# Zero rows of the second MoE stored during the first, another place for the partial block of two-block lists, and a tile moved 2 KB up

## The chip, the cores and the metric

The kernel runs on one core of a Trainium2 chip. The metric is the time of one execution in microseconds on the device. Lower is better. The core has a matrix engine (TensorE, PE in the profile), a vector engine (VectorE, DVE), a scalar engine (ScalarE, ACT), a general engine (GpSimd, POOL) and a queue engine that issues most transfers (SyncE, SP). The engines run side by side, each in the order of its own instructions, and wait for each other and for transfers through semaphores.

## The reference

Three stages, each on the output of the one before, all in fp32:

```python
# attention: q, k, v are [8 batches, 8 heads, 576, 64]
k_p, v_p = means of k and v over groups of 8 positions      # 72 of each
out = softmax(q @ k_p.T / 8) @ v_p
x = out as [4608 rows, 512]
# first MoE, then second MoE: 8 experts, w1 [8, 512, 1024], w2 [8, 1024, 512]
logits = x @ w_gate            # the second MoE adds modality_bias[modality_id]
e = argmax(logits); gate = softmax(logits)[e]
y = gate * (relu(x @ w1[e]) @ w2[e])
```

Each row is computed by one expert, the one that its logits pick. With the inputs given, experts 0 to 7 of the first MoE get 1018, 55, 333, 239, 827, 724, 24 and 1388 rows. In the second MoE experts 4 and 5 get 2286 and 2322 rows, the others none.

## The kernel before, in words

**Attention** runs over 40 steps (8 batches of 4 tiles of 128 rows and one of 64). Each finished tile is scattered by GpSimd, a row at a time, into a DRAM array `XS[0]`: eight areas of `CAP` = 4864 rows, one for each expert. An expert's list starts 256 rows into its area, and the 256 rows in front are zero. SP issues the loads of q, k and v ahead of the steps, and between them, by `zero_front` (line 92), the stores of those zero rows: one store of 256 rows (516 KB) for each expert and each MoE, at every second step from step 8 on, the first eight for `XS[0]`, the next eight for `XS[1]` (lines 674 and 675). The framework orders accesses to one DRAM array: a scatter to `XS[0]` waits for zero stores to `XS[0]` that were issued before it, and a zero store waits for scatters before it. Scatters among themselves are declared independent (line 172).

**An MoE** works through blocks of 256 rows (`moe_body`, line 904). A block reads its rows from `XS`, transposes them on VectorE (`xpose`), and splits them into a high and a low part (`split_x`, ScalarE and GpSimd) in the tile `xT`, or `xF` for the first block of each MoE. The weights of an expert are split in the same way: w1 into `w1h` (ScalarE) and `w1l` (VectorE for pieces 0 and 1, GpSimd for 2 and 3), w2 into `w2h` and `w2l`. GEMM 1 (line 284) makes eight pieces of 128 columns of h, each from 12 matmuls (high by high, high by low, low by high), into three PSUM buffers of two pieces; ScalarE writes the high part `hh` of two pieces, VectorE the low part `hl` (line 288). GEMM 2 (line 1075) makes the output in two halves of 128 rows with 24 matmuls each. In the first MoE the output of a block is at once multiplied with the second gate's weights: one product on VectorE for each half and expert (line 1157), part of it in the next block; then GpSimd scatters the rows into `XS[1]`. Hence `XS[1]` is filled during the first MoE, from its second block on.

Blocks are numbered from 0 here. **The partial block** of a list is the last one by position, with `count mod 256` rows; the rest of its 256 rows are other rows of the area, masked. If it has 128 rows or fewer, it is a **half block**: only one half is computed, with other code (`gemm1_half`, line 253: 48 matmuls, eight transposes, four `hl` pieces at line 273, and then 24 matmuls).

**The order of blocks** comes from a table that VectorE makes at run time (`table`, line 779) from the counts. The list that was longest after five batches goes first (expert 0); its first block is block 0. The others follow by number. `off` (line 843) is the position within a list at which its partial block stands, 0 or 1: 1 for the first list and for each list of more than one block. The code of a block is the same for every place; branches on bits of the table choose the half or full code and the splits of new weights. So the instructions in the program don't show the order, the table does. For the first MoE:

| block | 0 | 1 | 2 | 3 | 4 | 5 | 6 | 7 | 8 | 9 | 10 to 11 | 12 to 14 | 15 | 16 | 17 | 18 to 21 |
|---|---|---|---|---|---|---|---|---|---|---|---|---|---|---|---|---|
| expert | 0 | 0 | 0 | 0 | 1 | 2 | 2 | 3 | 4 | 4 | 4 | 5 | 6 | 7 | 7 | 7 |
| rows | 256 | 256 | 250 | 256 | 55 | 256 | 77 | 239 | 256 | 59 | 256 | 256, 212, 256 | 24 | 256 | 108 | 256 |
| code | full | full | full | full | half | full | half | full | full | half | full | full | half | full | half | full |

**Weights** of the next list are loaded into one staging tile (`stage`, w1 in one part, w2 in the other) as soon as the splits of the present list have freed it: w1 by four transfers of 512 KB at the end of the block before a list's first (`wload(0, nxt)`), w2 by one of 2 MB in the list's first block (`wload(1, i)`). All of them, the row loads (`ahead`, for the block after the next) and the zero stores stand in one queue, SP's. Where the block before a change of weights is full, its own code splits the next w1 and w2 between its matmuls (`next_w1`, `next_w2`). Where it is a half block, the splits come behind its GEMM 1 and at the start of the next block: pieces 0 and 1 of w1, then 2 and 3, `w2h`, and `w2l` in the next block's code, ahead of its `xpose` (lines 1004 to 1007 and 1033).

**Tiles in SBUF** stand one after the other in each partition, in the order in which the code asks for them; tiles named `edge` are gaps. By that layout `xT` begins at byte 172,032 of a partition, `xF` at 129,024.

Of the kernel before, what the change touches and what calls it, by code (L numbers as in the profile page):

```python
# [7 lines left out]
F32 = mybir.dt.float32  # L8
F32R = mybir.dt.float32r
# [3 lines left out]
ALU = mybir.AluOpType  # L13
# [7 lines left out]
def attn_moe_moe(ctx: ExitStack, tc: tile.TileContext, q, k, v, wg1, w1a, w2a, ids, wg2, bias2, w1b, w2b, out):  # L21
    nc = tc.nc
    ctx.enter_context(tc.manual_schedule())
    P = 128
# [5 lines left out]
    E = wg1.shape[1]  # L30
    FF = w1a.shape[2]
    NC1 = DM // P
    NC2 = FF // P
    BK = 256
# [17 lines left out]
    ZF = 8  # L52
# [37 lines left out]
    WT = dp.tile([E, DM], F32, name="WT")  # L90

    def zero_front(m, e):
        nc.sync.dma_start(
            out=XS[m][e * CAP : e * CAP + BK].rearrange("(p s) w -> p (s w)", p=P).rearrange("p (a w) -> p a w", a=4),
            in_=zero[:].unsqueeze(1).broadcast_to([P, 4, BK * XW // P // 4]))


    run = [ct([P, E], F32, f"run{m}") for m in range(2)]
# [56 lines left out]
    def gate_b2(oh, rk, ns, m, ib, rows, go=now, sc=None):  # L155
        pa = gtile(sc, 16, ns, E, "pa")
        go(lambda: nc.vector.tensor_tensor(out=pa, in0=rk[:, 0:ns, :], in1=run[m][:].unsqueeze(1).broadcast_to([P, ns, E]), op=ALU.add))
        go(lambda: nc.vector.tensor_tensor(out=run[m], in0=run[m], in1=rk[:, ns, :], op=ALU.add))
        go(lambda: nc.vector.tensor_tensor(out=pa, in0=pa, in1=oh[:, 0:ns, :], op=ALU.mult))
        pf = gtile(sc, 3, ns, 0, "pf")  # L160
        go(lambda: nc.vector.tensor_reduce(out=pf, in_=pa, op=ALU.add, axis=AX.X))
        pos = sp.tile([P, ns], I32, name=f"pos{ns}", tag=f"pos{ns}")
        go(lambda: nc.vector.tensor_tensor(out=pos, in0=pf, in1=ib, op=ALU.add))  # L163

        def scatter():
            def put(src, s):
                i = nc.gpsimd.indirect_dma_start(  # L167
                    out=XS[m][:], out_offset=bass.IndirectOffsetOnAxis(ap=pos[0 : src.shape[0], s : s + 1], axis=0),
                    in_=src, in_offset=None, bounds_check=E * CAP - 1, oob_is_err=False,
                )  # L170
                for o in scat[m]:
                    tc.declare_no_dep(i.ins, o.ins, reason="every row is written once")
                scat[m].append(i)

            rows(put)

        go(scatter)

    scat = [[], []]

    def pick_first(m):
        cnt = sp.tile([P, E], F32, name="pfc", tag="pfc")
# [401 lines left out]
    for i in range(len(T) + 2):  # L584
# [29 lines left out]
        if live:  # L614
# [48 lines left out]
            if i == 6:  # L663
# [7 lines left out]
                nc.vector.tensor_scalar(out=aux[:, :, :, 2:3], in0=aux[:, :, :, 1:2], scalar1=-1.0, scalar2=1.0, op0=ALU.mult, op1=ALU.add)  # L671
                for m in range(2):
                    nc.vector.tensor_copy(out=run[m], in_=ebase)
            if i >= ZF and (i - ZF) % 2 == 0 and (i - ZF) // 2 < 2 * E:
                zero_front((i - ZF) // 2 // E, (i - ZF) // 2 % E)
            if s == 1 and b >= 1:
                nc.gpsimd.tensor_copy(out=xr[(b - 1) % 2][:, :, DM + 1 : DM + 4], in_=aux[:, b - 1])
            if s == 0 and more:
# [74 lines left out]
    mp = ctx.enter_context(tc.tile_pool(name="moe", bufs=1, reuse_waits="tile"))  # L753
    mq = ctx.enter_context(tc.tile_pool(name="moep", bufs=1, space=PSUM, reuse_waits="tile"))
    my = ctx.enter_context(tc.tile_pool(name="moey", bufs=1, space=PSUM, reuse_waits="tile"))
    mp.tile([P, 176], F32, name="edge2")
    xT = mp.tile([P, 2, NC1, BK], F32R, name="xT")
    ring = [xr[0][:, 2:4], xr[1][:, 0:2], xr[1][:, 2:4]]
    tail = [xr[0][:, 0:2], ring[1]]

# [12 lines left out]
    invt = [mp.tile([P, NB, 2], F32, name=f"invt{m}") for m in range(2)]  # L773
    tab = [mp.tile([P, 4, NB], I32, name=f"tab{m}") for m in range(2)]
    nbt = [mp.tile([P, 5], I32, name=f"nbt{m}") for m in range(2)]
    hrow = mp.tile([P, 2, 2, BK], F32, name="hrow")
    yo = mp.tile([P, 2, DM], F32, name="yo")

    def table(m):
# [15 lines left out]
        V = nc.vector  # L795
# [4 lines left out]
        nb_ = t8("t_nb")  # L800
# [39 lines left out]

        off = t8("t_of")
        pp = t8("t_pp")
        V.scalar_tensor_tensor(out=off, in0=nb_, scalar=1.0, in1=is0[m], op0=ALU.is_gt, op1=ALU.max)
        V.tensor_tensor(out=pp, in0=start, in1=off, op=ALU.add)
        pd = t8("t_pd")
        V.scalar_tensor_tensor(out=pd, in0=nb_, scalar=-1.0, in1=off, op0=ALU.add, op1=ALU.subtract)
# [57 lines left out]
    def moe_body(m, i, full, chgn, hchg, phchg, slots, gate_prev, g1=None):  # L904
# [201 lines left out]
            next_w2(2, 3)  # L1106

        gemm2(1)
        if i == 1:
            regs[m] = load_regs(m)  # L1110
        if m == 0 and i > 0:
# [35 lines left out]
    revp = plx[:, 6 * E : 7 * E]  # L1147
    gsp = plx[:, 8 * E : 512]
    xq2 = mp.tile([P, BK // QP, P], F32, name="xq2")
    mt2 = mp.tile([P, 2, 4], F32, name="mt2")  # L1150
    V = nc.vector
    V.tensor_copy(out=revp, in_=rev)
    V.tensor_copy(out=biasp, in_=bias_t)
# [174 lines left out]
```

## Time and profile before

| | us |
|---|---|
| runs | 1168.77, 1168.18, 1159.60 |
| median | 1168.18 |
| profiled execution | 1167.45 |
| its span | 1165.6 |
| TensorE busy | 1080.1 (93%) |
| VectorE busy | 689.7 (59%) |
| GpSimd busy | 465.6 (40%) |
| ScalarE busy | 375.5 (32%) |

The span is the time from the first to the last instruction of the profiled execution; a little lies outside it. Busy times are of one engine, and the engines overlap. Line numbers (L284) are those of the kernel before. "A <- B" in a wait says that A's instruction began when B's had ended. A granted clock (PEclk) of 1.00 is 2.4 GHz, one of 0.50 is 1.2 GHz. In the names of the waits an engine's name with a q is its sequencer, which runs branches. The first MoE's blocks 3 to 10 lie between 297.18 and 477.93 us, and its 22 blocks end at 736.2 us.

### The profile page before, as it was taken

How to read it: one execution, taken by the hardware profiler on the slowest of the kernel's cores; microseconds unless marked ns; L12 is line 12 of the kernel's file. 1: busy time of each engine (PE TensorE's matmuls, PEld its weight loads, DVE VectorE, ACT ScalarE, POOL GpSimd, SP SyncE). 2: the span in 40 equal slices, each digit the busy share in tenths (PEclk: the TensorE clock that was granted, in tenths of full speed). 3: DMA queues.
4: the chain of work that ended last, by engine and by line, in shares of the span. 5: the costliest groups of instructions: out<-in, count | busy, mean ns of one | idle time of the engine just before them, and what ended most of it. 6: DMA issues, size and time to landing. Idle time of an engine off the chain costs nothing. (4 is left out here: it accounts for less than half of the span.)

```text
span 1165.6 us, 24589 instructions
## 1 busy us (share of the span) xinstructions
PE 1080.1 (93%) x6997; PEld 962.1 (83%) x6997; DVE 689.7 (59%) x1888; ACT 375.5 (32%) x717; POOL 465.6 (40%) x497
## 2 busy tenths in 40 slices
PE   7999989889988789999979998899999999999997
PEld 5888878778877678889768887888899899899996
DVE  4766676797897997898887777562212232212211
ACT  2454346332452432332622223222122242212221
POOL 6766887752372552351642234111211242221211
PEclk9999999989989899999989999999999999999999
DMA  8879999426285662171513621154111121121120
GB/s 214 216 194 227 252 288 272 171 57 164 57 227 156 167 183 62 38 205 39 155 63 74 167 65 39 41 139 137 54 58 38 40 63 48 37 65 47 38 66 32
DMA packets 148617, 135.61 MB, mean 116 GB/s; under 512 B 62502, under 2 KB 116774, under 8 KB 148272
## 3 DMA queue, kind: packets, MB, share of 16 engines
q1 hardware_dynamic: 138448, 104.68, 36.0%
q0 software_dynamic: 9424, 28.47, 6.8%
q8 instruction: 80, 1.31, 0.5%
q14 instruction: 137, 1.12, 0.3%
q10 hardware_dynamic: 528, 0.02, 0.0%
HBM read 249.30 MB, written 39.31 MB: 248 GB/s over the span
## 5 line engine op out<-in xcount | busy, mean ns | idle before, releaser
L284 PE MATMUL ph<-xT,w1h 128*128 128x256 f32 x2112 | 389.9, 288 | 25.0 <-DVE hl L288 14.7
L284 PEld LDWEIGHTS ph<-xT,w1h 128*128 128x128 f32 x2112 | 338.9, 197 | 31.6 <-DVE hl L288 15.7
L284 PE MATMUL ph<-xT,w1l 128*128 128x256 f32 x1056 | 303.8, 288 | 12.9 <-DVE w1l L228 11.2
L288 DVE SCALAR_TENSOR_TENSOR hl<-ph,hh 128x512 fp32r<-128x512 f32 x140 | 95.1, 685 | 266.0 <-ACT hh L287 230.2
L1075 PE MATMUL py<-w2h,hl 128*128 128x512 f32 x608 | 239.0, 393 | 8.5 <-DVEq L933 3.6
L1075 PE MATMUL py<-w2h,hh 128*128 128x512 f32 x608 | 240.0, 395 | 2.3 <-DVEq L933 1.2
L1075 PE MATMUL py<-w2l,hh 128*128 128x512 f32 x608 | 238.0, 391 | 0.6 <-POOL w2l L251 0.6
L241 POOL TENSOR_TENSOR xT<-xt,xT 128x512 fp32r<-128x512 f32 x78 | 101.6, 1321 | 335.8 <-ACT xT L240 335.4
L284 PEld LDWEIGHTS ph<-xT,w1l 128*128 128x128 f32 x1056 | 206.1, 195 | 14.0 <-DVE w1l L228 11.8
L1157 DVE SCALAR_TENSOR_TENSOR xr<-py,mt,wgt 128x512 f32<-128x512 f32 x284 | 195.4, 746 | 7.1 <-DVEq L933 6.6
L287 ACT ACTIVATE hh<-ph 128x512 fp32r<-128x512 f32 x140 | 83.6, 598 | 296.3 <-PE ph L284 262.4
L1075 PEld LDWEIGHTS py<-w2h,hl 128*128 128x128 f32 x608 | 114.6, 188 | 38.9 <-DVEq L933 5.3
L167 POOL DMA_INDIRECT XS<-xr,pos x84 | 83.4, 993 | 152.1 <-DVE pos L163 71.9
L1075 PEld LDWEIGHTS py<-w2h,hh 128*128 128x128 f32 x608 | 114.7, 189 | 24.7 <-DVEq L933 1.6
L1075 PEld LDWEIGHTS py<-w2l,hh 128*128 128x128 f32 x608 | 114.8, 189 | 22.9 <-POOL w2l L251 1.1
L1093 POOL DMA_INDIRECT out_dram<-yo,oi x37 | 37.2, 1005 | 132.2 <-POOLq L933 65.8
L335 POOL TENSOR_TENSOR stage<-stage 128x512 f32<-128x512 f32 (+4 forms) x60 | 70.3, 1182 | 15.2 <-DMA stage<-in_v_dram 8.0
L237 DVE STREAM_TRANSPOSE xt<-xq 128x1024 f32<-128x1024 f32 x42 | 52.2, 1244 | 38.1 <-POOL xT L241 19.8
L1091 ACT ACTIVATE yo<-py,mt 128x512 f32<-128x512 f32 x37 | 25.5, 690 | 146.5 <-PE py L1075 141.1
L1091 ACT ACTIVATE xr<-py,mt 128x512 f32<-128x512 f32 x39 | 26.8, 688 | 128.7 <-PE py L1075 121.9
L444 PE MATMUL psc<-kblk,qT 128*128 128x144 f32 (+1 forms) x320 | 52.8, 311 | 10.2 <-DVE asd L450 5.0
L228 POOL TENSOR_TENSOR w1l<-stage,w1h 128x1024 fp32r<-128x1024 f32 x22 | 53.9, 2470 | 6.9 <-ACT w1h L227 6.9
(291 smaller groups left out, 1352.2 us busy)
## 6 DMA issues: line engine op xcount, KB each, us to landing
stage<-in_moe_w_dram SPq DMA_DIRECT2D x196, 512.0 KB
stage<-in_moe_w_dram SPq DMA_DIRECT2D x44, 2048.0 KB
xq<-XS SPq DMA_DIRECT2D x180, 128.0 KB
XS<-zero SPq DMA_DIRECT2D x16, 516.0 KB
qp<-in_q_dram SPq DMA_DIRECT2D x32, 256.0 KB
stage<-in_k_dram SPq DMA_DIRECT2D x7, 1024.0 KB
stage<-in_v_dram SPq DMA_DIRECT2D x7, 1024.0 KB
wgt<-WT SPq DMA_DIRECT2D x1, 2048.0 KB
```

What stands on the lines that cost most here:

```text
L167: i = nc.gpsimd.indirect_dma_start(out=XS[m][:], out_offset=bass.IndirectOffsetOnAxis(ap=pos[0 : src.shape[0], s : s + 1], axis=0), in_=sr ...
L228: (eng or nc.vector).tensor_tensor(out=w1l[:, j], in0=wst1[:, :, f], in1=w1h[:, j].bitcast(F32), op=ALU.subtract)
L237: nc.vector.transpose(out=dst[:].rearrange("p c (g i) -> p g c i", i=QP), in_=src[:].rearrange("p g (c j) -> p g c j", c=NC1))
L241: (eng or nc.gpsimd).tensor_tensor(out=dst[:, 1, cs], in0=src[:, cs], in1=dst[:, 0, cs].bitcast(F32), op=ALU.subtract)
L284: nc.tensor.matmul(ph[:, fc % 2, :], lhsT=lw[:, fc // 2, c, fs], rhs=rx, start=n == 0, stop=n == len(mms) - 1)
L287: nc.scalar.activation(out=hh[f2], in_=ph, func=AF.Relu)
L288: nc.vector.scalar_tensor_tensor(out=hl[f2], in0=ph, scalar=0.0, in1=hh[f2][:].bitcast(F32), op0=ALU.max, op1=ALU.subtract)
L335: (eng or nc.gpsimd).tensor_tensor(out=r[0:pp, sl, 0:w], in0=r[0:pp, sl, 0:w], in1=r[0:pp, sl, w : 2 * w], op=ALU.add)
L444: nc.tensor.matmul(ps[0:tk, hp // 2, (hp % 2) * 2 * KP : (hp % 2 + 1) * 2 * KP], lhsT=qT[:, hp, 0:tk], rhs=kb[:, hp, :], start=True, stop= ...
L1075: nc.tensor.matmul(py, lhsT=lw[fc // 2][:, fc % 2, s * P : (s + 1) * P], rhs=rw[fc // 2][:, fc % 2, :], start=n == 0, stop=n == 3 * NC2 - 1)
L1091: nc.scalar.activation(out=x2[:, s, 0:DM], in_=py, func=AF.Copy, scale=t_[:, s, 0:1])
L1157: V.scalar_tensor_tensor(out=junk[e % 2], in0=py, scalar=sc, in1=wgt[:, e, :], op0=ALU.mult, op1=ALU.mult, accum_out=lgz[:, s, e : e + 1])
```

## The change

Three things. The zero stores for `XS[1]` leave attention: blocks 2 to 9 of the first MoE issue one each, behind the first half of GEMM 2 in the code. Those for `XS[0]` are issued at every third step from step 8 on. Zero stores and scatters are declared independent of each other, since no row is written by both. In the table `off` is 1 only for the first list and for lists of more than two blocks (the first list's own first block is not counted). And the small tile `mt2` is asked for earlier, the gap `edge2` shrinks from 176 to 160 elements and stands behind the small tiles, and `xT` behind it, so that `xT` begins at byte 174,080; the tiles behind it move by 32 bytes.

```diff
     def zero_front(m, e):
-        nc.sync.dma_start(
+        i = nc.sync.dma_start(
             out=XS[m][e * CAP : e * CAP + BK].rearrange("(p s) w -> p (s w)", p=P).rearrange("p (a w) -> p a w", a=4),
             in_=zero[:].unsqueeze(1).broadcast_to([P, 4, BK * XW // P // 4]))
+        for o in scat[m]:
+            tc.declare_no_dep(i.ins, o.ins, reason="no row is put in front of an expert's list")
+        zer[m].append(i)
+
+    scat = [[], []]
+    zer = [[], []]
...
-                for o in scat[m]:
+                for o in scat[m] + zer[m]:
                     tc.declare_no_dep(i.ins, o.ins, reason="every row is written once")
...
-    scat = [[], []]
...
-            if i >= ZF and (i - ZF) % 2 == 0 and (i - ZF) // 2 < 2 * E:
-                zero_front((i - ZF) // 2 // E, (i - ZF) // 2 % E)
+            if i >= ZF and (i - ZF) % 3 == 0 and (i - ZF) // 3 < E:
+                zero_front(0, (i - ZF) // 3)
...
-    mp.tile([P, 176], F32, name="edge2")
-    xT = mp.tile([P, 2, NC1, BK], F32R, name="xT")
...
+    mt2 = mp.tile([P, 2, 4], F32, name="mt2")
+    mp.tile([P, 160], F32, name="edge2")
+    xT = mp.tile([P, 2, NC1, BK], F32R, name="xT")
...
-        V.scalar_tensor_tensor(out=off, in0=nb_, scalar=1.0, in1=is0[m], op0=ALU.is_gt, op1=ALU.max)
+        V.scalar_tensor_tensor(out=off, in0=nb_, scalar=2.0, in1=is0[m], op0=ALU.is_gt, op1=ALU.max)
...
         gemm2(1)
+        if m == 0 and 2 <= i < 2 + E:
+            zero_front(1, i - 2)
...
-    mt2 = mp.tile([P, 2, 4], F32, name="mt2")
```

With the counts above the new table of the first MoE differs from the old one in blocks 5 and 6 alone: block 5 is expert 2's half block of 77 rows, block 6 its full block. The table of the second MoE is the same. The code of the blocks stands in the same order as before but for the zero stores.

SP's queue in attention, around the second zero store. `XS_86` is `XS[0]`, `zero` the tile of zeros, `qp` a q tile; a semaphore `DMASW` is that of a scatter, `DMAHW` that of an earlier transfer of SP's own. Before:

```order
L93 DMA XS_86<-zero 512x1x258 [waits DMAHW6_49]
L416 DMA qp<-in_q_dram 64x8x64 [waits DMAHW7_49,PE_49]
L416 DMA qp<-in_q_dram 128x8x64 [waits DMAHW0_49,PE_49]
L324 DMA stage<-in_v_dram 128x4x512 [waits DMAHW1_49,Pool_49]
L325 DMA stage<-in_v_dram 64x1x512 [waits DMAHW2_49,Pool_49]
L93 DMA XS_86<-zero 512x1x258 [waits DMAHW3_49,DMASW4_49]
```

With the change:

```order
L93 DMA XS_86<-zero 512x1x258 [waits DMAHW6_49]
L420 DMA qp<-in_q_dram 64x8x64 [waits DMAHW7_49,PE_49]
L420 DMA qp<-in_q_dram 128x8x64 [waits DMAHW0_49,PE_49]
L328 DMA stage<-in_v_dram 128x4x512 [waits DMAHW1_49,Pool_49]
L329 DMA stage<-in_v_dram 64x1x512 [waits DMAHW2_49,Pool_49]
L420 DMA qp<-in_q_dram 128x8x64 [waits DMAHW3_49,PE_49]
L93 DMA XS_86<-zero 512x1x258 [waits DMAHW4_49]
```

The second zero store comes one q tile later, and its wait for a scatter is gone.

SP's queue at the end of block 3 of the first MoE: the last of the four transfers of w1, and the row loads (`xq`) of block 4's code. `XS_87` is `XS[1]`. Before:

```order
L210 DMA stage<-in_moe_w_dram 32x4x1024
L1116 REGISTER_ALU
L1116 COMPARE_AND_BRANCH
L933 UNCONDITIONAL_BRANCH x4
L202 TENSOR_LOAD tab_2936
L202 ISA x2
L233 ISA
L233 DMA xq_79<-XS_86 32x8x128
```

With the change:

```order
L214 DMA stage<-in_moe_w_dram 32x4x1024
L93 DMA XS_87<-zero 512x1x258
L1123 REGISTER_ALU
L1123 COMPARE_AND_BRANCH
L938 UNCONDITIONAL_BRANCH x4
L206 TENSOR_LOAD tab_2926
L206 ISA x2
L237 ISA
L237 DMA xq_79<-XS_86 32x8x128
```

A zero store stands between the load of w1 and the row loads; the codes of blocks 2 to 9 each got one at this place.

## Rows read from the trace of the kernel before

**Rows 1.** Busy times of attention's stretch: from:to, length, engines (instructions), PEclk, DMA share, GB/s.

```profile
0.00:210.90 210.90, 190.45 (x1351) 163.26 (x1351) 137.12 (x441) 96.23 (x253) 153.96 (x233) 0.99 0.92 236
```

**Rows 2.** Waits of TensorE and SP from 0 to 211 us: in total, times, longest.

```profile
PE psc L444 <- DVE asd L450: 5.0, 3, 1.7
...
PE pq L429 <- DMA qp<-in_q_dram: 0.8, 1, 0.8
...
SPq L93 <- DMA XS<-xr,pos: 36.6, 3, 15.6
```

**Rows 3.** Busy times (PE, PEld, DVE, ACT, POOL) of blocks 3 to 8, 10 and 16.

```profile
297.18:319.59 22.41, 22.41 (x148) 20.32 (x147) 19.26 (x58) 10.91 (x15) 9.19 (x7) 1.00 0.12 27
319.59:333.21 13.62, 12.78 (x84) 10.78 (x83) 13.18 (x32) 8.62 (x15) 8.50 (x6) 1.00 1.06 277
333.21:368.20 34.99, 27.33 (x148) 24.80 (x148) 30.47 (x70) 10.08 (x15) 17.09 (x11) 0.85 0.72 204
368.20:381.82 13.62, 12.78 (x84) 10.79 (x83) 10.72 (x30) 8.50 (x15) 4.29 (x4) 1.00 0.16 38
381.82:415.94 34.12, 26.23 (x147) 22.59 (x148) 30.75 (x70) 14.18 (x19) 20.50 (x13) 0.90 0.66 160
415.94:441.17 25.23, 22.91 (x148) 20.21 (x147) 23.29 (x62) 6.80 (x11) 10.66 (x7) 1.00 0.76 209
455.02:477.93 22.91, 22.35 (x148) 20.05 (x148) 17.63 (x66) 4.42 (x9) 6.65 (x7) 1.00 0.27 78
581.15:617.37 36.22, 26.77 (x147) 24.24 (x148) 30.18 (x71) 10.67 (x16) 17.07 (x11) 0.86 0.26 84
```

**Rows 4.** TensorE's timeline in blocks 5 and 7: start, length, instruction, [idle <- releaser].

```profile
337.21 0.58 PE L284 MATMUL ph<-xT,w1l 128*128 128x256 f32 x1 [3.52 <-DVE w1l L228]
...
352.63 0.50 PE L284 MATMUL ph<-xT,w1h 128*128 128x256 f32 x2 [4.13 <-DVE hl L288]
...
386.07 0.58 PE L284 MATMUL ph<-xT,w1l 128*128 128x256 f32 x1 [3.78 <-DVE w1l L228]
...
399.31 0.52 PE L284 MATMUL ph<-xT,w1h 128*128 128x256 f32 x2 [2.42 <-DVE hl L288]
```

**Rows 5.** VectorE's timeline in blocks 3 to 5, and its products from the page.

```profile
307.48 2.36 DVE L228 TENSOR_TENSOR w1l<-stage,w1h 128x1024 fp32r<-128x1024 f32 x2 [0.24 <-ACT w1h L227]
...
326.73 1.60 DVE L273 TENSOR_TENSOR hl<-pt,hh 128x256 fp32r<-128x256 f32 x4
...
334.42 6.06 DVE L228 TENSOR_TENSOR w1l<-stage,w1h 128x1024 fp32r<-128x1024 f32 x2 [0.22 <-issue]
...
343.94 6.90 DVE L251 TENSOR_TENSOR w2l<-stage,w2h 128x1024 fp32r<-128x1024 f32 x2 [0.90 <-DVEq L1116]
350.77 1.23 DVE L237 STREAM_TRANSPOSE xt<-xq 128x1024 f32<-128x1024 f32 x1
...
L1157 DVE SCALAR_TENSOR_TENSOR xr<-py,mt,wgt 128x512 f32<-128x512 f32 x284 | 195.4, 746 | 7.1 <-DVEq L933 6.6
```

**Rows 6.** Timelines of SP at the end of block 3 and of ScalarE around 333.

```profile
317.37 2.87 SPq L210 DMA_DIRECT2D stage<-in_moe_w_dram  x4
...
330.70 3.89 ACT L227 CAST w1h<-stage 128x1024 fp32r<-128x1024 f32 x4 [2.00 <-DMA stage<-in_moe_w_dram]
...
337.87 3.89 ACT L244 CAST w2h<-stage 128x1024 fp32r<-128x1024 f32 x4 [2.70 <-DMA stage<-in_moe_w_dram]
```

**Rows 7.** Busy times behind the two stops in block 5.

```profile
337.20:343.30 6.10, 6.09 (x28) 6.09 (x29) 5.54 (x16) 4.49 (x5) 3.64 (x3) 0.50 0.25 49
353.70:357.00 3.30, 3.30 (x18) 3.30 (x17) 2.76 (x8) 0.00 (x0) 0.00 (x0) 0.50 1.13 256
```

**Rows 8.** PE and PEld of GEMM 1 alone: blocks 0 (first MoE), 4 and 3 (second).

```profile
216.27:219.10 2.83, 2.83 (x24) 2.83 (x24) 1.00 0.50 190
824.41:835.72 11.31, 11.31 (x96) 11.26 (x95) 1.00 0.07 25
802.53:813.50 10.97, 10.97 (x96) 10.94 (x96) 1.00 0.22 55
```

## The prediction

> **What bounds the kernel now.** I read the stretches of the run first: attention (0 to 210.90 us) keeps TensorE busy for 190.45 us of 210.90, with the DMA engines at a share of 0.92 [rows 1]. TensorE sets the pace, so I look for the places where it does not run. In attention the list of waits shows that nothing it waits for is a transfer, but for 0.8 us of a q tile; its longest wait is VectorE's (`asd`, 5.0 us in three pieces). SP stood for 36.6 us, in three pieces, behind scatters before it could store zero rows [rows 2].
>
> Then the first MoE, block by block [rows 3]. A full block takes 22.41 us when nothing is late (block 3), a half block 13.62 us (block 4), and a full block behind a half one of the same list 22.91 us (block 10). Three blocks stand out: 5, 7 and 16 take 34.99, 34.12 and 36.22 us, which is 12.6, 11.7 and 13.8 us over 22.41. Each is the first block of a list and follows a half block that ends the list before. Block 8, the first of a list behind a list of one block, takes 25.23 us, 2.8 over. Inside blocks 5 and 7 TensorE stops twice [rows 4]: for VectorE's low part of w1 (3.52 and 3.78 us) and then for VectorE's `hl` (4.13 and 2.42 us). In a half block the splits of the next weights do not fit. Ahead of block 4, a change behind a full block, two low parts of w1 took VectorE 2.36 us; ahead of block 5 they took 6.06 us, with GpSimd's at the same time, and the two low parts of w2 behind them 6.90 us [rows 5]. Weights also come late there: ScalarE waited 2.00 us for w1 and 2.70 us for w2 [rows 6]. At block 7 the weights are not what is late: the two stops are VectorE's.
>
> **The change part by part.**
>
> *The order of blocks.* The new comparison touches lists that have exactly two blocks in the table. Of the lists given there is one: expert 2 of the first MoE, 333 rows, a full block and one of 77 rows. Blocks 5 and 6 trade places: half, then full. The second MoE has lists of nine table blocks each and keeps its order. The change from expert 2 to 3 then stands behind a full block; the change from expert 1 to 2 stays behind a half one.
>
> New block 5 (half) starts at 333.2, as before, and meets the same splits. VectorE ends the low parts of w1 at 334.42 + 6.06 = 340.5, those of w2 at 343.94 + 6.90 = 350.8, and the transpose at 352.0 [rows 5]. Only then comes the first of the four `hl` pieces (1.60 us together), so the second GEMM gets going at 352.4. TensorE's 48 matmuls of GEMM 1 and its transposes are through some 4 us earlier and do not decide. Of the second GEMM's 24 matmuls 22 are left. A full block's 48 take 22.41 - 11.31 = 11.1 us [rows 3, 8], so 0.23 each: 5.1 us. Before it TensorE has been idle for about 4 us. After the stop of 3.52 us its granted clock was 0.50, the lower level (1.2 GHz), for 6.1 us, and after that of 4.13 us for 3.3 us [rows 7]. I take the second, the nearer in length and in cause; half of 3.3 us is lost, 1.6 us. Block 5 ends at 359.1, and block 6 starts about 0.5 us later, the difference between blocks 10 and 3, at 359.6.
>
> Block 6 (full) is like block 10 behind block 9: 22.9 - 0.5 = 22.4 us, to 382.0. Its splits for expert 3 go as ahead of block 4, where there was no stop. Block 7 (full, one block in its list): the load of expert 4's w1 is issued when the splits have freed the stage. That was 20.2 us after block 3 started (317.37 - 297.18), and the data took 13.3 us to ScalarE (330.70 - 317.37) [rows 6]. So 359.6 + 20.2 + 13.3 = 393.1. The block's sixth eighth of GEMM 1 is done at 390.5 and the last `hl` is wanted at about 397.4 (382.0 + 11.3 + 18 matmuls of 0.23); two casts and two subtractions from 393.1 (1.9 + 2.4 us, the casts by half of the 3.89 us for four) just fit. Block 7 takes 22.4 us, to 404.4. Block 8 took 25.23 us behind a late block 7; between 22.41 and 25.23 I take 23.8, since w2 of expert 4 is still the next thing to be late. Block 9 starts at 428.2 instead of 441.17 [rows 3]: **13.0 us less**.
>
> The ends: the second GEMM of block 5 all at the lower level (+3.5), block 8 as before (+1.4) and block 7 with the 2.8 us that block 8 loses now behind a list of one block give 5.3 us less; no clock loss and block 8 at 22.41 give 16.0 us less.
>
> *Eight zero stores leave attention, and eight stay without waits.* What goes: 8 stores of 516 KB and SP's 36.6 us, and the scatters' waits for zero stores. Behind the waiting SP stood q and k/v loads, but TensorE waited 0.8 us for one [rows 2], so what hides them is the loads' lead. Between 0 and 3 us of gain; I take 0.5, since VectorE's chain ends the waits there.
>
> *Eight zero stores come to blocks 2 to 9.* Each is one more issue on SP, ahead of the row loads for two blocks later, and 516 KB at the 277 GB/s of block 4 [rows 3] is 1.9 us. The one that matters is issued in block 3, behind w1 of expert 2 (317.37) and ahead of its w2 [rows 6], where the DMA share is 1.06: w2 lands at about 339.8 instead of 337.9. New block 5 wants it on VectorE at 343.9, so this is covered by the low parts of w1; without that cover it costs 1.9 us. The store of block 6 lies between w1 and w2 of expert 4 and is the reason why I leave block 8 at 23.8. The others meet loads that have a block or more to spare. 0 to +2 us; I take 0.5.
>
> *The transposed rows' tile.* `xT` moves from byte 172,032 of a partition (84 times 2 KB) to 174,080 (85 times). No operation changes. `xF`, the tile of the first blocks, lies at 129,024, 63 times 2 KB, an odd multiple too: its 24 matmuls took 2.83 us, 118 ns each, and 96 with `xT` took 11.31 us, 118 ns, or 10.97 us after a stop, 114 ns [rows 8]. So I take 0. The ends: 0.34 us for each of the 33 full blocks that read `xT` (11 us) either way.
>
> *The constant, the small tiles' new places:* no work, no wait on an engine that is waited for.
>
> **Sum:** 1167.45 (the profiled execution) - 13.0 - 0.5 + 0.5 = 1154.5 us, and I say 1155. That execution lies 0.7 us under the median of the runs shown, 1168.18.
>
> **The rivals.**
>
> (a) *Only part comes through:* new block 5 loses more to the clock and the loads of experts 3 and 4, one list of one block behind another short one, are late next. For it: blocks 5, 7 and 8 are in a stretch where DMA shares are 0.66 to 1.06 [rows 3]. Against: DMA stood at a share of 0.12 to 0.16 in blocks 3 and 6. 1159 to 1165.
>
> (b) *Attention gains more than 3 us,* because its DMA share is 0.92 and eight stores of 1.9 us, 15 us of transfers, go. Against: the waits of rows 2. 1147 to 1152.
>
> (c) *`xT`'s new place speeds GEMM 1 up* to 114 ns in all blocks: 11 us more, 1144. Against: `xF` at an odd multiple.
>
> (d) *Slower:* two half blocks in a row leave VectorE behind, and block 6 stops as block 7 did. VectorE in new block 5: after 352.0 there are `hl` (1.6), eight products for the gate of the block before (195.4 us for 284, so 5.5) [rows 5] and small operations, 3.5 us by the gap between 340.5 and 343.9, then the transpose: 363.9 for block 6's first `hl`. TensorE runs out of its three buffers when 72 matmuls of block 6 are done, at 359.6 + 8.5 = 368.1. The margin is 4.2 us; if VectorE is later than that, the stop moves to block 6. Then blocks 5 to 8 take 13.6 + 13.8 + 34.1 + 22.4 + 25.2, with 1.9 for a zero store: 111.0 against 108.0 now, so 1170.5.
>
> (e) *The clock stays low longer:* if the lower level lasts 6.1 us, as behind the stop of 3.52 us, the whole second GEMM of new block 5 runs at it and takes 5.1 us more, not 1.6: 1158.5. For it: this time the stop comes behind a GEMM that was itself interrupted. Against: the like stop in block 5 now. The Trainium skill, "TensorE: Matmul & The Clock Gate", section "HAM oscillation — how this bites in real kernels", has a rule for this: idle gaps between groups of matmuls bring the clock down, and each group then starts cold. By that rule the time is (e)'s; the trace agrees in part, since after the stop of 4.13 us the lower level came, but a microsecond late and for 3.3 us.
>
> (f) *It does not do what it says:* no list changes its order or the stop at block 7 belongs to its own one-block list, and time stays within 3 us of 1167. Against: at block 7 no transfer is waited for.
>
> **How the numbers follow.** About 1%, 11.7 us, is what a measurement of this kernel can tell from no change; that is 1156.5 downward and 1179.9 upward. The case as worked out, 1151.5 to 1157.5: 0.50; (a) 0.18; (b) 0.08; (c) 0.04; (d) 0.05; (e) 0.10; (f) 0.05. The range of 1147 to 1167 holds the main case, (a), (b), (e) and half of (f), about 0.88; it takes in 1148.5 to 1164, the ends of the order's term (16.0 and 5.3 us) together with those of attention and the zero stores, and the other cases beside them. Faster by over 1%: 0.37 of the main case, (b) and (c): 0.49. Within 1%: the rest of the main case, (a), (e), (f) and nearly all of (d), whose price is 0.3%: 0.49. Slower by over 1%: 0.02, a (d) that costs more than it is priced at.
>
> **What would show it.** Right: a half block stands at 333 to 360 and a full one without a stop behind it, and blocks begin at about 333, 360, 382, 404 and 428; no wait of SP for scatters before a zero store; `hl` in block 6 on time. Wrong: a wait of TensorE for `hl` or the low part of w1 in block 6 or 7; a start of block 9 later than 436; a GEMM 1 with `xT` off 11.0 to 11.3 us; w2 of expert 2 landing after 344; attention ending earlier than 207.

## The result

| | before | changed |
|---|---|---|
| runs | 1168.77, 1168.18, 1159.60, 1168.89 | 1152.59, 1146.39, 1142.62, 1147.27 |
| median | 1168.47 | 1146.83 |
| profiled execution | 1167.45 | 1152.59 |

The ratio is 0.9848, 95% interval [0.9801, 0.9895]: 21.6 us less by the medians, where 13 were forecast. The median lies 0.2 us under the low end of the range. The profiled execution is the slowest of the four; the sums below are made against it. Two executions of the kernel before, beside e5 to e8, took over 2650 us and are left out of the times and ratios here.

**The profile of the changed kernel.** Line numbers are 4 to 6 higher than before (GEMM 1 is L288, its half form L264, GEMM 2 L1080). Attention's stretch (columns as in [rows 1]) and two waits of it:

```profile
0.00:205.21 205.21, 187.26 (x1352) 160.53 (x1352) 137.04 (x441) 96.10 (x253) 153.19 (x233) 0.99 0.82 222
```

```profile
PE psc L448 <- DVE asd L454: 4.6, 3, 1.6
...
SPq L237 <- DMA XS<-xr,pos: 5.4, 1, 5.4
```

Attention ends 5.7 us earlier, with the DMA share at 0.82 instead of 0.92, and SP waits for no scatter ahead of a zero store any more; the wait for VectorE's `asd`, which I took for attention's bound, is nearly what it was [rows 1, 2].

Blocks 3 to 8, 10 and 16 (columns as in [rows 3]):

```profile
291.86:314.26 22.40, 22.40 (x148) 20.31 (x147) 19.23 (x57) 10.91 (x15) 9.21 (x7) 1.00 0.19 39
314.26:328.13 13.87, 12.77 (x85) 10.79 (x83) 13.43 (x32) 8.71 (x15) 8.47 (x6) 1.00 1.06 260
328.13:355.41 27.28, 18.30 (x84) 15.09 (x84) 25.04 (x55) 9.88 (x17) 16.03 (x9) 0.75 0.97 274
355.41:377.49 22.08, 22.08 (x148) 19.99 (x148) 17.79 (x55) 10.31 (x15) 11.18 (x9) 1.00 0.36 106
377.49:401.97 24.48, 23.17 (x149) 20.08 (x147) 22.75 (x60) 12.79 (x17) 16.29 (x10) 1.00 0.90 233
401.97:427.93 25.96, 24.22 (x149) 21.90 (x147) 22.79 (x61) 6.80 (x11) 10.49 (x7) 0.93 0.82 223
441.77:464.65 22.88, 22.35 (x148) 20.06 (x148) 17.60 (x66) 4.43 (x9) 6.63 (x7) 1.00 0.38 101
568.13:603.18 35.05, 26.50 (x148) 24.00 (x149) 29.98 (x71) 10.54 (x16) 17.05 (x11) 0.85 0.27 88
```

Block 5 is now the half block. Blocks 5 to 8 take 99.8 us (328.13 to 427.93) instead of 108.0 (333.21 to 441.17): 8.2 us less, where 13.0 were forecast. Block 16, which the change does not touch, keeps its loss.

Block 5 stops twice, as the half block of the forecast (TensorE's timeline, columns as in [rows 4]; behind it the busy times after the two stops, as in [rows 7]):

```profile
332.03 0.58 PE L264 MATMUL ph<-w1l,xT 128*128 128x256 f32 x1 [3.55 <-DVE w1l L232]
...
347.00 0.79 PE L1080 MATMUL py<-w2h,hl 128*128 128x512 f32 x1 [4.12 <-DVE hl L277]
```

```profile
332.00:338.20 6.20, 5.79 (x25) 5.50 (x26) 5.54 (x16) 2.60 (x3) 3.75 (x3) 0.50 0.61 211
347.00:351.90 4.90, 4.90 (x12) 3.84 (x13) 4.90 (x16) 0.93 (x3) 2.66 (x3) 0.50 1.19 233
```

VectorE's chain in blocks 5, 7 and 8 (start, length, instruction, idle time before):

```profile
338.74 6.74 DVE L255 TENSOR_TENSOR w2l<-stage,w2h 128x1024 fp32r<-128x1024 f32 x2 [0.89 <-ACT w2h L248]
345.41 1.23 DVE L241 STREAM_TRANSPOSE xt<-xq 128x1024 f32<-128x1024 f32 x1
...
378.17 2.35 DVE L255 TENSOR_TENSOR w2l<-stage,w2h 128x1024 fp32r<-128x1024 f32 x2
...
389.19 3.46 DVE L232 TENSOR_TENSOR w1l<-stage,w1h 128x1024 fp32r<-128x1024 f32 x2
...
402.86 4.57 DVE L255 TENSOR_TENSOR w2l<-stage,w2h 128x1024 fp32r<-128x1024 f32 x2
...
410.48 1.25 DVE L241 STREAM_TRANSPOSE xt<-xq 128x1024 f32<-128x1024 f32 x1 [0.36 <-DMA stage<-in_moe_w_dram]
```

The same two subtractions take 2.35 us at the start of block 7 and 4.57 us at the start of block 8. GpSimd splits beside them in both. What differs is which engine starts first; here is VectorE's second subtraction and GpSimd's first, at block 7 and then at block 8:

```profile
379.31 1.22 DVE L255 TENSOR_TENSOR w2l<-stage,w2h 128x1024 fp32r<-128x1024 f32 x1
379.40 3.39 POOL L255 TENSOR_TENSOR w2l<-stage,w2h 128x1024 fp32r<-128x1024 f32 x1 [1.73 <-ACT w2h L248]
...
403.88 2.47 POOL L255 TENSOR_TENSOR w2l<-stage,w2h 128x1024 fp32r<-128x1024 f32 x1 [2.81 <-ACT w2h L248]
404.00 3.43 DVE L255 TENSOR_TENSOR w2l<-stage,w2h 128x1024 fp32r<-128x1024 f32 x1
```

In each pair the one that starts first, by about 0.1 us, takes its usual time, and the other takes 1 to 2 us more.

### The profile page after: what moved, and what is told of

The parts are those of the page before. It is cut to its first block, busy times and chain, and to the rows that moved or that the text cites. A ratio compares the mean times of both kernels' runs of the same rounds, so it can differ in the third digit from the quotient of the medians.

```text
span 1150.8 us, 24573 instructions
## 1 busy us (share of the span) xinstructions
PE 1075.5 (93%) x6997; PEld 958.1 (83%) x6997; DVE 682.0 (59%) x1888; ACT 375.5 (33%) x717; POOL 464.9 (40%) x497
## 5 line engine op out<-in xcount | busy, mean ns | idle before, releaser
L288 PE MATMUL ph<-xT,w1h 128*128 128x256 f32 x2112 | 382.3, 284 | 16.4 <-DVE hl L292 7.4
L288 PEld LDWEIGHTS ph<-xT,w1h 128*128 128x128 f32 x2112 | 332.6, 193 | 22.5 <-DVE hl L292 8.3
L288 PE MATMUL ph<-xT,w1l 128*128 128x256 f32 x1056 | 299.9, 284 | 5.5 <-DVE w1l L232 3.8
L1080 PE MATMUL py<-w2h,hl 128*128 128x512 f32 x608 | 240.0, 395 | 12.6 <-DVE hl L277 4.1
L1080 PE MATMUL py<-w2h,hh 128*128 128x512 f32 x608 | 241.1, 397 | 2.1 <-DVEq L938 1.2
L1080 PE MATMUL py<-w2l,hh 128*128 128x512 f32 x608 | 238.7, 393 | 0.0
L288 PEld LDWEIGHTS ph<-xT,w1l 128*128 128x128 f32 x1056 | 202.0, 191 | 6.1 <-DVE w1l L232 4.0
L1080 PEld LDWEIGHTS py<-w2h,hl 128*128 128x128 f32 x608 | 115.1, 189 | 42.9 <-DVE hl L277 6.7
L1080 PEld LDWEIGHTS py<-w2h,hh 128*128 128x128 f32 x608 | 115.3, 190 | 24.8 <-DVEq L938 1.6
L1080 PEld LDWEIGHTS py<-w2l,hh 128*128 128x128 f32 x608 | 115.4, 190 | 22.1
L255 POOL TENSOR_TENSOR w2l<-stage,w2h 128x1024 fp32r<-128x1024 f32 x20 | 53.0, 2667 | 11.4 <-ACT w2h L248 10.8
```

The source lines that it names most:

```text
L255: (eng or nc.vector).tensor_tensor(out=w2l[c], in0=wst2[:, 2 * c : 2 * c + 2, :], in1=w2h[c][:].bitcast(F32), op=ALU.subtract)
L288: nc.tensor.matmul(ph[:, fc % 2, :], lhsT=lw[:, fc // 2, c, fs], rhs=rx, start=n == 0, stop=n == len(mms) - 1)
L1080: nc.tensor.matmul(py, lhsT=lw[fc // 2][:, fc % 2, s * P : (s + 1) * P], rhs=rw[fc // 2][:, fc % 2, :], start=n == 0, stop=n == 3 * NC2 - 1)
```

## The experiments

Each was timed beside the kernel before on the same chip; e1 to e4 shared one chip (before: 1162.94 us), e5 to e8 another (1161.33), e9 to e11 a third (1162.77).

**e1, the order alone.**

```diff
-        V.scalar_tensor_tensor(out=off, in0=nb_, scalar=1.0, in1=is0[m], op0=ALU.is_gt, op1=ALU.max)
+        V.scalar_tensor_tensor(out=off, in0=nb_, scalar=2.0, in1=is0[m], op0=ALU.is_gt, op1=ALU.max)
```

> The kernel before with the new comparison alone (half block of expert 2 ahead of its full block). Theory A (the three parts add up, as the trace of the changed kernel reads: about 8 us from the order, about 4 us from the zero stores, nothing from the place of the transposed rows' tile): blocks 5 to 8 take 99 to 101 us together instead of 108.0, attention as long as before (209 to 212 us), the whole 7 to 9 us less, ratio 0.992 to 0.994. Theory B (the prediction's size: 13.0 us from the order; the zero stores in blocks 3 to 6 took the rest back): blocks 5 to 8 take 95 us, 13 us less, ratio 0.989. Theory C (the order saves nothing by itself): ratio over 0.997.

1154.29 us, ratio 0.9911 [0.9878, 0.9945]. Blocks 5 to 8 take 99.4 us (333.75 to 433.19), as theory A had it; C falls. The interval takes in B's ratio, but the blocks decide: 8.5 us less, not 13.

**e2, the zero stores' part alone:** the independence, and the stores' new places.

```diff
+        for o in scat[m]:
+            tc.declare_no_dep(i.ins, o.ins, reason="no row is put in front of an expert's list")
...
-                for o in scat[m]:
+                for o in scat[m] + zer[m]:
...
-            if i >= ZF and (i - ZF) % 2 == 0 and (i - ZF) // 2 < 2 * E:
+            if i >= ZF and (i - ZF) % 3 == 0 and (i - ZF) // 3 < E:
...
+        if m == 0 and 2 <= i < 2 + E:
+            zero_front(1, i - 2)
```

> The kernel before with the zero stores' part alone: eight stores for the second MoE's array move from attention to blocks 2 to 9, zero stores and scatters are independent, the others at every third step. Theory A: attention gets 3 to 6 us shorter, since SP's 36.6 us of waits ahead of q, k and v loads and 4 MB of stores are gone; ratio 0.995 to 0.997. Theory B (the shorter attention in the one profile is chance from run to run, part of it stands ahead of the first zero store): ratio 0.999 to 1.000, and attention between 209 and 212 us.

1150.63 us, ratio 0.9907 [0.9878, 0.9936]: 12.3 us less by the medians, more than theory A said. B falls. Not all of it need lie in attention: block 16, which this part does not touch, took 30.36 us in e2's profile and 36.22 before. Here is what the kernel before does and this one doesn't. First GpSimd's first scatter of a batch, and TensorE behind it, in e1 (attention as in the kernel before) and, below, in e2:

```profile
92.09 1.04 POOL L167 DMA_INDIRECT XS<-xr,pos  x1 [6.29 <-DVE lgt L499]
...
104.39 0.66 PE L356 MATMUL pk<-ident,kvp 128*128 128x128 f32 x4 [0.97 <-POOL kvp L347]
110.50 0.63 PE L369 MATMUL pv<-ident,kvp 128*64 128x128 f32 x4 [1.16 <-POOL kvp L349]
```

```profile
88.95 1.04 POOL L173 DMA_INDIRECT XS<-xr,pos  x1 [2.20 <-DVE pos L169]
```

GpSimd idled 6.29 us before the scatter in e1 and 2.20 us in e2. The view names a VectorE reduction that the scatter does not read; its positions had been there since 87.75 us. That it waited for the declared order is shown by e5 below, where the order alone goes and the wait is 2.19 us. GpSimd's sums of k and v stand behind the scatters, and TensorE waited for them twice. Second, the end of attention, in e1 (timelines of SP, ScalarE and TensorE, and the busy times behind the stop):

```profile
168.18 3.44 SPq L93 DMA_DIRECT2D XS<-zero  x1
...
180.19 11.43 SPq L223 DMA_DIRECT2D stage<-in_moe_w_dram  x4
...
193.12 1.99 ACT L227 CAST w1h<-stage 128x1024 fp32r<-128x1024 f32 x2 [8.21 <-DMA stage<-in_moe_w_dram]
...
196.28 2.29 PE L444 MATMUL psc<-kblk,qT 128*128 128x144 f32 x8 [6.07 <-ACT qT L431]
```

```profile
196.00:200.00 4.00, 3.72 (x16) 3.68 (x17) 1.29 (x2) 3.63 (x7) 4.00 (x4) 0.50 1.05 395
```

ScalarE casts the first expert's w1 between its copies for attention. The weights land late in a stretch full of zero stores, ScalarE stands 8.21 us on them, TensorE 6.07 us on ScalarE's `qT`, and then it runs at the lower clock. In e2 ScalarE waited 2.95 us there and TensorE 0.81. But e1's is the worst case: e3 below, with the same attention, had 5.35 and 3.2 us, and the kernel before, whose ScalarE came later, 1.74 and 0.3.

**e3, the tiles' places alone.**

```diff
-    mp.tile([P, 176], F32, name="edge2")
-    xT = mp.tile([P, 2, NC1, BK], F32R, name="xT")
...
+    mt2 = mp.tile([P, 2, 4], F32, name="mt2")
+    mp.tile([P, 160], F32, name="edge2")
+    xT = mp.tile([P, 2, NC1, BK], F32R, name="xT")
```

> The kernel before with the new places of the tiles alone (transposed rows from byte 174,080 on). Theory A: no time, ratio 0.998 to 1.002, a first GEMM of 96 matmuls still takes 11.3 us at a place where nothing stopped before it. Theory B (the place is what brings the rest of the time that the sum of order and zero stores leaves open): ratio 0.990 to 0.996, with shorter first GEMMs or shorter transposes or splits that write this tile.

1165.09 us, ratio 1.0027 [1.0006, 1.0048], a little over theory A's 1.002, away from B. That it is 2 us slower by the medians has no cause that a row shows. Full blocks take 22.41 us in the first MoE and 22.21 in the second, as before. B falls.

**e4, the changed kernel again,** with no edit.

> The changed kernel itself again, on the same chip as the parts. Theory A (the parts add up): its gain is the sum of the gains of the three parts run beside it, within 3 us, ratio 0.981 to 0.988. Theory B (the parts need each other): its gain is over 5 us more than that sum. The profile is a second look at attention: by theory A its end lies at 204 to 208 us again; if it is chance, anywhere up to 211.

1141.71 us, ratio 0.9827 [0.9793, 0.9861], 21.2 us less; the three parts beside it make 8.65 + 12.31 - 2.15 = 18.8: within 3 us, theory A. Attention ends at 199.60 us, earlier than A's 204. Blocks 5 to 8 take 95.9 us; block 5 took 24.29 here, since its two low parts of w2 took VectorE 4.55 us instead of 6.74:

```profile
332.81 4.55 DVE L255 TENSOR_TENSOR w2l<-stage,w2h 128x1024 fp32r<-128x1024 f32 x2 [0.89 <-DVEq L1123]
```

In e4 VectorE began 0.46 us ahead of GpSimd's first (332.81 and 333.27), in the changed kernel's first profile 0.06 us behind it (338.74 and 338.68). The code is the same; the two subtractions are 2.2 us shorter, and block 5 is 3.0 us shorter.

**e5 and e6, the zero stores' part in two.** e5 has only e2's first two pieces, the declared independence; all stores stay. e6 moves only the eight stores (and declares them, which are for `XS[1]`, independent of that array's scatters):

```diff
-            if i >= ZF and (i - ZF) % 2 == 0 and (i - ZF) // 2 < 2 * E:
-                zero_front((i - ZF) // 2 // E, (i - ZF) // 2 % E)
+            if i >= ZF and (i - ZF) % 2 == 0 and (i - ZF) // 2 < E:
+                zero_front(0, (i - ZF) // 2)
...
+        if m == 0 and 2 <= i < 2 + E:
+            zero_front(1, i - 2)
```

> The kernel before with the independence of zero stores and scatters alone; all 16 stores stay in attention, at every second step. The whole part took 12 us off (e2). Theory W (the waits: GpSimd's scatters stood up to 6.85 us behind zero stores, its sums of k and v behind them came late, and TensorE stopped 1.2 us a batch): the 12 us come from here, ratio 0.989 to 0.993, attention ends near 201 us. Theory T (the transfers: eight stores of 516 KB less between 128 and 200 us, where the DMA share is about 1.0): ratio 0.998 to 1.001. Theory M (both, as the steps of e2 against those of the kernel before divide it: 4.0 us by 138 us, 6 us after): ratio 0.996 to 0.998, 4 us less by the 26th step, nothing after.

> The kernel before with the eight stores for the second MoE's array moved to blocks 2 to 9 alone (independent of that array's scatters); the stores for the first array stay at every second step and keep their waits, and so do its scatters. Theory W: ratio 0.997 to 1.000. Theory T: ratio 0.989 to 0.993. Theory M: ratio 0.993 to 0.996, with the TensorE stops of 1.2 us up to 127 us still there and those from 147 us on gone.

e5: 1155.43 us, ratio 0.9944 [0.9913, 0.9975]. e6: 1154.90 us, ratio 0.9944 [0.9918, 0.9970]. By the medians these are 5.9 and 6.4 us less. W and T fall as the whole cause, since each was to bring all of it in one run and next to nothing in the other; M has the halves, though e5 gains more than it said. Together they make 12.3 us, as much as e2, so the wider spacing of the first array's stores adds nothing that can be seen. Attention ends at 204.37 us in e5 (W had said 201) and at 200.82 in e6. The stretch from 140 to 200 us in e1, e3 (the same attention), e5, e6 and e2, one row of each (columns as in [rows 1]):

```profile
140.00:200.00 60.00, 53.34 (x393) 46.41 (x393) 40.81 (x134) 28.78 (x73) 46.62 (x53) 0.95 1.03 268
```

```profile
140.00:200.00 60.00, 56.21 (x407) 49.08 (x406) 41.10 (x136) 30.96 (x78) 49.82 (x54) 0.94 1.05 279
```

```profile
140.00:200.00 60.00, 56.36 (x415) 48.65 (x412) 42.61 (x143) 32.11 (x82) 50.33 (x54) 0.97 0.93 257
```

```profile
140.00:200.00 60.00, 58.12 (x442) 49.99 (x440) 45.77 (x154) 34.37 (x87) 52.62 (x55) 1.00 0.81 228
```

```profile
140.00:200.00 60.00, 57.85 (x440) 49.78 (x439) 45.53 (x154) 34.35 (x87) 52.25 (x55) 1.00 0.72 207
```

With eight stores less (e6, e2) the DMA share is lower and TensorE does 440 matmuls or more here instead of 393 to 415. In e5 TensorE still stopped 3.00 us for ScalarE behind w1, as in e3; in e6 0.24 us. ScalarE began on w1 at 187 to 193 us in the four runs with all stores in attention and at 184 to 187 in e2, e4, e6 and the changed kernel (later, at 188 to 191, in e9 to e11, whose attention ran late for another reason, told at the end). But e6 kept the late scatters, and one of its rows names what they wait for:

```profile
91.12 1.04 POOL L174 DMA_INDIRECT XS<-xr,pos  x1 [6.32 <-DVE lgt L504]
...
113.92 1.04 POOL L174 DMA_INDIRECT XS<-xr,pos  x1 [2.17 <-DMA XS<-zero]
```

TensorE waited 1.00 and 1.14 us behind them, as in e1, and not at all in e5. These two waits are 2.1 of the 5.9 us that e5 gains. Where the rest lies is not shown; block 16, which e5 does not touch, took 32.33 us in its profile.

**e7, single half lists through the full code.** Their blocks count as longer than 128 rows where the code is chosen:

```diff
+        l2 = lst
+        V.memset(l2, 0.0)
+        V.tensor_tensor(out=l2[:, 0 : NB - 1], in0=ch[:, 0 : NB - 1], in1=ch[:, 1:NB], op=ALU.mult)
+        V.scalar_tensor_tensor(out=l2, in0=l2, scalar=float(BK), in1=ll, op0=ALU.mult, op1=ALU.add)
...
-        V.scalar_tensor_tensor(out=fm, in0=ll, scalar=float(P), in1=pw2, op0=ALU.is_gt, op1=ALU.mult)
+        V.scalar_tensor_tensor(out=fm, in0=l2, scalar=float(P), in1=pw2, op0=ALU.is_gt, op1=ALU.mult)
...
```

> The changed kernel, and a list of one block of 128 rows or fewer (experts 1 and 6 of the first MoE) goes through the full code, whose own splits then cover the change of weights. Theory A (the loss belongs to a change of weights behind a half block): block 4 takes 22.4 us instead of 13.9, block 5 13.6 to 13.9 instead of 24.3 to 27.3, block 15 22.4 instead of 13.8, block 16 22.4 to 23 instead of 35; 5 to 7 us less than the changed kernel, ratio to the kernel before 0.976 to 0.979. Theory B (the loss belongs to the loads of short lists: the next weights come late whichever code runs): blocks 5 and 16 keep over 4 us of it each, and the full code's 8.6 us more for each of two blocks make it 5 us or more slower than the changed kernel, ratio 0.987 or more.

1143.31 us, ratio 0.9846 [0.9806, 0.9886]: neither. Blocks 4 and 5, 15 and 16:

```profile
332.80:350.54 17.74, 14.72 (x84) 11.99 (x83) 16.69 (x39) 6.70 (x13) 8.81 (x6) 0.90 1.07 282
309.56:332.80 23.24, 22.75 (x149) 20.16 (x147) 21.49 (x58) 12.69 (x17) 15.09 (x10) 1.00 0.90 249
```

```profile
547.76:572.25 24.49, 23.25 (x149) 20.06 (x147) 21.55 (x58) 12.79 (x17) 14.99 (x10) 1.00 0.79 214
572.25:597.22 24.97, 22.87 (x148) 20.21 (x147) 22.60 (x63) 7.01 (x12) 10.80 (x8) 1.00 0.24 69
```

Block 16's loss of 12.6 us is gone, but blocks 15 and 16 together take 49.5 us, as in the changed kernel (48.9). In these two neither TensorE nor ScalarE waits for a transfer; all waits of TensorE are for VectorE.

**e8, the zero stores in blocks 9 to 16.**

```diff
-        if m == 0 and 2 <= i < 2 + E:
-            zero_front(1, i - 2)
+        if m == 0 and 9 <= i < 9 + E:
+            zero_front(1, i - 9)
```

> The changed kernel with the eight zero stores in blocks 9 to 16 instead of 2 to 9. Theory A (the 2 us that blocks 7 and 8 are over the forecast each come from VectorE and GpSimd, which split at the same time behind the loads of a one-block list, and only a little from the stores): blocks 5 to 8 take 95 to 99 us instead of 95.9 to 99.8, the time within 2 us of the changed kernel. Theory B (the stores ahead of the weights in the queue are what makes blocks 7 and 8 late): block 7 takes 22.4 us and block 8 23.8, 3 to 5 us less than the changed kernel, ratio to the kernel before 0.978 to 0.980.

1144.78 us, ratio 0.9848 [0.9805, 0.9891]. Blocks 7 and 8 take 23.65 and 25.95 us, blocks 5 to 8 99.4, 0.4 over theory A's range; block 8 is as late as with the stores (25.96), and B falls: the stores are not what delays these two.

**e9, e10, e11.** e10 is the changed kernel with `next_w2` splitting every low part of w2 on GpSimd; e9 is e10 and e7 together; e11 is the changed kernel without the tiles' new places.

```diff
-                gated(nxt_chg(), lambda: gated(live, lambda: [split_w2(c, nc.gpsimd if c in LOP else None) for c in cs]))
+                gated(nxt_chg(), lambda: gated(live, lambda: [split_w2(c, nc.gpsimd) for c in cs]))
```

> The changed kernel without the new places of the tiles (order and zero stores alone). Theory A (the place is worth nothing): ratio to the kernel before as the changed kernel's, 0.981 to 0.986. Theory B (the place helps in company, though alone it measured 1.0027): ratio 0.988 or more.

> The changed kernel with all four low parts of w2 split by GpSimd where a full block splits them (before, VectorE had two of the four). Theory V (VectorE is what makes blocks 7 and 8 late: in block 8 its two low parts of w2 take 4.57 us beside GpSimd's, then its transpose and the first pieces of the low part of h come late and TensorE stops 1.7 us): block 8 takes 22.4 to 23.5 us instead of 25.0 to 26.0, block 7 22.4 to 24.5, the whole 2 to 4 us less than the changed kernel, ratio to the kernel before 0.978 to 0.982. Theory L (the loads of the weights make them late): blocks 7 and 8 as before or longer, since GpSimd takes 9.5 us for four low parts; ratio 0.983 or more.

> Both: single half lists through the full code (e7) and all low parts of w2 on GpSimd. Theory V: block 5 (half) 13.9 to 16 us instead of 17.7, block 15 22.4 to 24.5 instead of 24.5, block 16 22.4 to 23.5 instead of 25.0, block 8 22.4 to 23.5; 4 to 8 us less than e7, ratio to the kernel before 0.976 to 0.981. Theory L: as e7 or slower, ratio 0.984 or more.

e11: 1148.13 us, ratio 0.9875 [0.9837, 0.9914], between the theories. Alone the places measured 0.3% slower; taken away, 0.3 to 0.5% slower too, against the changed kernel's ratios on other chips. The two contradict each other and no row shows the places, so their worth stays open within half a per cent. e10: 1144.89 us, ratio 0.9849 [0.9809, 0.9890], 3.2 us under e11 beside it, from which it differs by the tiles' places too. Its ratio lies over V's range and within L's, and is no better than the changed kernel's 0.9848: the whole time does not decide. Attention ended late in its profile, at 208.47 us (e11: 208.71; more on that below), which the edit does not touch. The blocks do decide. Its blocks 8 and 7, and GpSimd's four low parts:

```profile
400.13:422.54 22.41, 22.41 (x149) 20.32 (x148) 18.38 (x58) 6.80 (x11) 14.57 (x10) 1.00 1.02 277
377.43:400.13 22.70, 22.70 (x149) 20.24 (x148) 19.59 (x58) 12.70 (x17) 18.93 (x12) 1.00 0.89 232
```

```profile
400.52 9.53 POOL L255 TENSOR_TENSOR w2l<-stage,w2h 128x1024 fp32r<-128x1024 f32 x4
```

Block 8 is down to the pace of an undisturbed one with the loads where they were: theory V by its blocks, and L, which had them as before or longer, falls. e9: 1141.80 us, ratio 0.9824 [0.9791, 0.9857], the best of its chip, 6.3 us under e11. Blocks 4 to 8 take 105.8 us (113.7 in the changed kernel), 15 and 16 46.3 (48.9). Those are V's blocks, but for block 5, which at 13.62 us is even shorter; the ratio misses V's 0.976 to 0.981. So it beats the changed kernel in the sum of these blocks; by the ratio to the kernel before (0.9824 against 0.9848 and 0.9827) the two cannot be told apart.

## Why the prediction held, and where not

The time came out near the range's low end by two misses that partly cancel, and that is luck. Blocks 5 to 8 gained less than forecast and attention more: block 5 began 5 us earlier than forecast (328.13 for 333.2), and yet block 9 at 427.93, where 428.2 was forecast.

**The order (13.0 forecast; 8.2 in the profile, 8.5 in e1, 12.0 in e4).** The mechanism was right. Block 5 was to take 26.4 us to the next start and took 27.28, 27.06 and, in e4, 24.29; VectorE's transpose was to end 18.8 us after its start and ended 18.5 after; block 6 was to take 22.4 and took 22.08. The step in it that failed is the price of blocks 7 and 8: 22.4 and 23.8 forecast, 24.48 and 25.96 measured (23.4 to 24.5 and 25.0 to 26.1 in the other runs with their lists), some 4 us. I took the loads for what is late there, and for two subtractions 2.4 us, their time with nothing beside them; they took 3.46 in block 7 and 4.57 in block 8. e8 moved the stores out of their way and brought no gain; e10 took the two low parts of w2 from VectorE and brought block 8 to 22.41. A block between two changes of weights has both splits on VectorE, and one that starts behind GpSimd's takes up to 3.4 us instead of 1.2. The term's spread from 8.2 to 12.0 is mostly block 5, by the same cause (e4).

**The clock in block 5.** The lower level lasted 4.9 us behind the second stop, between the 3.3 taken and the 6.1 of rival (e). GEMM 1 was at it too for 6.2 us, which cost nothing, VectorE being later. The Trainium skill, "TensorE: Matmul & The Clock Gate", section "HAM oscillation — how this bites in real kernels", has the rule that (e) goes by: groups behind idle gaps start cold. The trace agrees at both stops, with a granted clock of 0.50 from 332.00 and from 347.00 us on. The price lies between the two cases.

**Attention (0.5 forecast, 0 to 3 as its range; 5.7 in the profile, 12.3 for the whole part in e2).** This is the step that failed: that what SP has queued is hidden by the loads' lead and that VectorE ends attention's waits. I had seen the scatters' waits for zero stores and gave them no price, because the view put GpSimd's idle time down to VectorE; and I did not ask what the first weights land behind. Attention ended at 205.21 us, earlier than the 207 that the forecast gave as a sign of being wrong. Of the 5.7 us, 1.8 stand ahead of the first zero store and are no part of the change; the profile of the changed kernel is its slowest run, 5.8 us over the median. From VectorE's reduction in step 8, where the first zero store is issued, to the MoE's first GEMM it is 154.6 us before and 150.6 after; on the chip of e1 to e4 155.2 and 151.2 with the old attention (e1, e3) and 144.6 and 144.7 with the new (e2, e4). So 4.0 to 10.6 us of the gain can be seen in attention. What I had as rival (b), 0.08, for its DMA share, is about half of the part's 12.3 us (e6); the other half, the declared order (e5), was in no rival.

**Zero stores in the MoE (0.5, 0 to 2).** Right, by single profiles: blocks 3 to 10 take 181.2 us in e2, which has the stores and the old order, and 180.7 before. In the changed kernel w2 of expert 2 came later, and VectorE, still at the low parts of w1, began on it 10.6 us into the block instead of 10.7 [rows 3, 5]:

```profile
335.60 3.89 ACT L248 CAST w2h<-stage 128x1024 fp32r<-128x1024 f32 x4 [5.60 <-DMA stage<-in_moe_w_dram]
```

**The tile's place (0).** Right as far as can be told, which is to half a per cent of the time; GEMM 1 with `xT` still runs at 118 ns for each matmul [rows 8], 0.06 us more for the 96 than before and so just outside the 11.0 to 11.3 us of the forecast's signs:

```profile
809.83:821.20 11.37, 11.37 (x96) 11.26 (x95) 1.00 0.08 27
```

**The sum.** The order's term was 1 to 5 us too large and attention's 3 to 12 us too small; the two partly cancelled. The rivals: (a)'s loss at blocks 7 and 8 came, by another cause; (d) did not, `hl` is on time in block 6; (c) and (f) fall. Of the signs of being wrong, a wait for the low part of w1 in block 7 came too, 0.4 us long. (d)'s sum holds 13.8 us that are none of its four blocks' times and that the prediction does not explain; nothing else rests on it.

## What to carry over

An order declared between two writers of one array can cost time even where the fast engine never waits for a load: follow it to every engine that writes the array, and distrust an idle time that is put down to an instruction whose result the waiting one doesn't read. Where an engine casts weights between the steps of another stage, price what lands in front of those weights. Before blaming loads for a late block, compare one instruction's length in the good and the bad place, and see which engine's started first. And compare two profiles of the same code before reading a gain from one: block 5 of the same kernel took 27.28 and 24.29 us.

## What the runs showed of the hardware

An fp32 subtraction of two SBUF tiles on VectorE took 1.22 us alone or when it started ahead of GpSimd's, and 3.4 us when it started just behind one; GpSimd's took 2.4 to 2.5 us when first and 3.4 when just behind. The Trainium skill, "SBUF — State Buffer", section "SBUF: two separate sides", has the two engines share one pair of ports for such operations: whichever starts first holds it for the whole instruction, and the other is blocked. The trace agrees, by the two pairs of rows under the result; the figures are the trace's.

Block 16, behind a half block, goes with the same order of starts in the eleven profiles whose edits leave its splits alone. Where GpSimd's first low part of w1 started ahead of VectorE's (before, the changed kernel, e1, e3, e4, e6, e8: by 0.03 to 0.65 us), it took 34.9 to 36.2 us. Where VectorE's was first (e2, e5, e10, e11: by 0.03 to 0.58 us), it took 28.0 to 32.3. No run changed this order by itself, so that it makes the whole difference is not shown.

Another page of the Trainium skill, "Perfetto Trace Analysis", section "Optimizing Scalar/DVE Operations", warns that moving work between those two might not help; here it did, 9.53 us of GpSimd for block 8's 2.6 to 3.5 us.

One thing stays open. In the profiles of before and after, and in e9 to e11, TensorE stops three to five times for 1.0 to 1.7 us behind VectorE or ScalarE between 40 and 180 us; in e1 to e8 it never does. In the changed kernel's profile ScalarE and VectorE begin within 0.1 us of each other, 2.1 and 2.5 us after the TensorE results that they read were there:

```profile
142.19 0.58 ACT L474 COPY pt<-ppt 128x512 f32<-128x512 f32 x1 [5.18 <-PE pav L484]
...
142.10 0.76 DVE L452 TENSOR_REDUCE amx<-psc 128x8 f32<-128x576 f32 x1 [3.22 <-PE pav L484]
...
143.87 1.22 PE L448 MATMUL psc<-kblk,qT 128*128 128x144 f32 x8 [1.55 <-DVE asd L454]
```

So the `asd` wait that the prediction took for attention's bound is of this kind. It goes with the chip or the occasion, not with the change, and no view shows what the two wait for.
